# A wider second channel layer, computed in two parts, and a new order for stores and VectorE's work

## The chip, the cores and the metric

The kernel runs on one core of a Trainium2 chip. The metric is the device time of one execution in microseconds (us); lower is better. A core has TensorE (matmuls, "PE" in the profile), VectorE ("DVE"), ScalarE ("ACT"), GpSimd ("POOL") and SyncE ("SP", which here only issues DMA transfers).

## What is computed

Attention with a threshold for 8 batches and 8 heads, and behind it an MLP mixer. Everything is float32.

```python
# q, k, v: (8, 8, 576, 64); per batch and head
scores = (q @ k.T) / 8
thresh = scores.max(-1) - tau
scores = where(scores >= thresh, scores, -1e9)
attn = softmax(scores)
x = concat over heads of (attn @ v)          # (8, 576, 512), rows are tokens
# mixer: w_tok1 (576, 256), w_tok2 (256, 576), w_ch1 (512, 1536), w_ch2 (1536, 512)
h = relu(x.T @ w_tok1) @ w_tok2              # over tokens, per batch
u = x + h.T
out = u + relu(u @ w_ch1) @ w_ch2            # over channels, per token
```

The first channel layer is the product with w_ch1, the second channel layer the one with w_ch2. Adding u at the end is the residual.

## The kernel before

**Rows and rounds.** A batch is a row (b = 0 to 7). Attention is cut into units of 128 queries; two units make a round. A round is: scores on TensorE (L825, 24 passes of 64-row matmuls), row maxima on VectorE (L842, `mx`), the bias from them on GpSimd (L848), masks on ScalarE (L858), exponentials on ScalarE (L868), sums and reciprocals on VectorE (L276, L277), scaling on GpSimd (L285), a 32x32 block transpose of e on VectorE (L315, `T`), and four transfers on SP that bring the blocks to their places (L327, the "moves of e"). For three units the values (L365, L370) multiply with v.

**The mixer of the row before lies between.** While the attention of row b+1 runs, TensorE fills the time with the mixer of row b: transposes of x (L435), token layers (L454 and L472), then for one group of 256 tokens (two in row 0, none in row 7) the first channel layer (L948, 12 visits of 8 passes) and the second (L964, 2 x 4 visits of 24 passes). A float32 matmul shows as two passes. What is left of each row goes to DRAM (L531, "spill") and is computed in delayed groups at the end (L1309), where attention is over.

**Banks.** Token and channel visits, values and transposes share two PSUM banks (`m0`, `m1`). A visit takes a free bank, and an engine copies, clips or adds the result out of it; then the bank is free again. For the first channel layer this is a relu on ScalarE (L953) or VectorE (L956). For the second channel layer of rows 1 to 7 it is an add of the residual on VectorE (L978), for row 0 a copy on ScalarE (L984).

**The residual.** In rows above 0 the tokens of a group lie permuted and transposed. `turn_u` (L933, two transposes on VectorE) writes u into the tile `us`, eight transfers (`move_u`, L940) bring it to the tile `ut`. Then `us` is written a second time, by the adds `us = bank + ut`, and stored (L988), one transfer for each 128 tokens. `us` has one buffer: the next group's `turn_u` waits until both stores of the group before have landed.

**The order** is made when the program is built. A small planner (`Scheduler`) holds one clock for each engine and takes at each step the operation that can start earliest; among those that can start now, the one with the lower `rank`, then the older one. Each operation has a fixed cost; a transfer's landing is reckoned from the bytes at 214 KB per us and 1.5 us. Scores of later rounds are held back until as much mixer work is done as is due (`plan`, `done`). The planner only writes each engine's instruction list; on the chip each engine works strictly through its list and waits for semaphores.

Of the kernel before, what the change touches and what calls it, by code (L numbers as in the profile page):

```python
# [21 lines left out]
def kernel(  # L22
# [523 lines left out]

    TOKEN_RANK, TOKEN_AFTER_TOKEN = 1.5, 2.5
    SLACK, SPARE = 1.0, 4.0
    FLIGHT, RATE, LANDING = 8, 214.0, 1.5
    WARM_UNTIL, WARM_GAP, WARM_TURN = 110.0, 0.6, 0.11  # L550

    class Op:

        def __init__(self, eng, cost, fn, deps, after, rank, lag, row, index):
            self.eng, self.cost, self.fn, self.rank, self.lag, self.row, self.index = eng, cost, fn, rank, lag, row, index
            self.end, self.bank, self.frees, self.later, self.open, self.other = None, None, None, [], 0, None
            self.dmas, self.landed, self.shared = None, None, False
            self.deps = [d for d in deps if d is not None]
            for d in self.deps + [d for d in after if d is not None]:
                if d.end is None:  # L560
                    d.later.append(self)
                    self.open += 1
# [5 lines left out]
    class Scheduler:  # L568
# [22 lines left out]
        def banked(self, cost, work, on, cost_out, leave, deps=(), rank=5, row=None, rank_out=0, other=None):  # L591
# [3 lines left out]
            y.frees = x  # L595
            return x, y

        def sure(self, x):
            t = max([d.landed + SPARE if d.landed else d.end + d.lag + SLACK * (d.eng != x.eng) for d in x.deps] + [0.0])
            if x.bank:  # L600
                t = max(t, min(b.free for b in self.banks if b.free is not None) + SLACK)
            return t

        def start(self, x, eng):
            t = max([d.landed or d.end + (d.lag if d.eng != eng else 0.0) for d in x.deps] + [0.0])
            if x.dmas and len(self.in_flight) == FLIGHT:
                t = max(t, self.in_flight[0])
            if x.shared and eng == "dve":
                t = max(t, self.clock["pool"])
            if x.bank:  # L610
                frees = [b.free for b in self.banks if b.free is not None]
                if not frees:
                    return None
                t = max(t, min(frees))
            return max(t, self.clock[eng])
# [46 lines left out]
        def run(self, until):  # L662
            while not until():
                best = None
                for e in self.clock:
                    c = self.pick(e)
                    if c and (best is None or c[0][0] < best[0][0]):
                        best = c + (e,)
                if best is None:
                    assert all(x.end is not None for x in self.ops), [(x.eng, x.rank, x.index, x.open) for x in self.ops if x.end is None][:20]  # L670
                    return
                _, t, x, eng = best
                if eng == "pe" and t < WARM_UNTIL:
                    self.keep_warm(t)
                self.ready[x.eng].remove(x)
                if x.other:
                    self.ready[x.other[0]].remove(x)
                    if eng != x.eng:
                        x.eng, x.cost, x.fn = x.other
                if x.dmas:  # L680
                    x.end = self.transfer(t, *x.dmas)
                    x.landed = self.in_flight[-1]
                else:
                    x.end = t + x.cost
                self.clock[x.eng] = x.end
                if x.eng == "pe":
                    self.last_rank = x.rank
                if x.bank:
                    b = min((b for b in self.banks if b.free is not None), key=lambda b: b.free)
                    b.free = None  # L690
                    x.bank = b, b.pool.tile([P, MAIN], F32, tag=b.tag, name=f"bank_{x.index}")
                    x.fn(x.bank[1])
                    if x.row is not None:
                        self.done += x.cost
                elif x.frees:
                    b, tile_ = x.frees.bank
                    x.fn(tile_)
                    b.free = x.end + 0.15
                else:
                    x.fn()  # L700
                for y in x.later:
                    y.open -= 1
                    if not y.open:
                        self.enter(y)
# [214 lines left out]
    def make_groups(b, halves):  # L919
        uT = xTs[b]  # L920
        reads = []
        for i in range(NOW[b]):
# [32 lines left out]
            def relu_v(bank, j, s=s):  # L955
                nc.vector.tensor_scalar(out=s["g"][:, j, 0:n], in0=bank[:, 0:n], scalar1=0.0, scalar2=None, op0=ALU.max)  # L956

            def ch2(bank, t, c, s=s, i=i):
                to = bank[:, 0:P]
                t0 = GR * i + P * t  # L960
                if not b:
                    nc.tensor.matmul(to, lhsT=uT[:, c, t0 : t0 + P], rhs=ident, is_transpose=True, start=True, stop=False, skip_group_check=True)
                for j in range(NJ):
                    nc.tensor.matmul(  # L964
                        to,
                        lhsT=s["g"][:, j, P * t : P * t + P],
                        rhs=wc2[:, j, P * c : P * c + P],
                        start=(j == 0 and b > 0),
                        stop=(j == NJ - 1),
                        skip_group_check=True,  # L970
                    )

            def leave(bank, t, c, s=s):
                if not b and "us" not in s:
                    new_us(s)
                o = s["us"][:, t].rearrange("q a x -> q (a x)")[:, P * c : P * c + P]
                if b:
                    nc.vector.tensor_add(  # L978
                        out=o.rearrange("q (k d) -> q k d", k=4),
                        in0=bank[:, 0:P].rearrange("q (k d) -> q k d", k=4),  # L980
                        in1=s["ut"][:, t][:, :, 32 * c : 32 * c + 32],
                    )
                else:
                    nc.scalar.copy(out=o, in_=bank[:, 0:P])  # L984
# [5 lines left out]
            have = halves["20"] + (halves["21"] if i else [])  # L990
            moved = []
            if b:
                turn = sched.op("dve", 1.2, turn_u, have + state["stores"] + state["adds"] + (converted if b == 1 else []), 5)
                reads.append(turn)
                moved = [sched.op("sp", 1.2, lambda k=k, m=move_u: m(k), (turn,), 1, dmas=(nt, 53, 0.645)) for k in range(4)]
            relus = []
# [15 lines left out]
            seconds, stores, adds = [], [], []  # L1012
            for t in range(nt):
                outs = []
                for c in range(NCC):
                    x, y = sched.banked(
                        2.7 if b else 2.8,
                        lambda bank, t=t, c=c, f=ch2: f(bank, t, c),
                        "dve" if b else "act",
                        0.21,  # L1020
                        lambda bank, t=t, c=c, f=leave: f(bank, t, c),
                        relus + moved + (converted if not b else []) + (state["stores"] if not b else []),
                        2,
# [4 lines left out]
                    seconds.append(x)  # L1028
                    if not b:
                        reads.append(x)  # L1030
                    fills[b] = fills.get(b, 0.0) + x.cost
                adds += outs
                stores.append(sched.op("sp", 0.35, lambda t=t, f=store: f(t), outs, 2, dmas=(1, 150, 0.35)))
            state["ch2"], state["stores"], state["adds"] = seconds, stores, adds
        return reads

# [451 lines left out]
```

## Time and profile before

| | |
|---|---|
| median of 3 runs | 1270.09 us (1269.9 to 1276.9) |
| the profiled execution's own time | 1273.39 us |
| its span, first to last instruction | 1271.4 us |
| mean granted TensorE clock | 0.991 |
| TensorE busy / VectorE / ScalarE / GpSimd | 97% / 59% / 44% / 25% |
| second channel layer, matmuls (L964) | 1536 passes of 128 columns, 181.4 us busy |
| first channel layer, matmuls (L948) | 768 passes of 256 columns, 181.0 us busy |
| adds out of the bank (L978) | 48 of 128x128, 275 ns each |
| `turn_u` (L933) | 12 transposes, 1088 ns each |
| stores of groups and delayed groups (L988 and others), 256 KB | 32, 2.1 us from issue to landing in the median |

The profile is of one execution. Its page gives each engine's busy time, the groups of instructions by line of the kernel with count and mean duration, and who waited for whom. Busy time of TensorE is modelled at the ends of matmuls, so that the distance between two starts says more than the duration of one. The 16 stores at L988 are those of rows 0 to 6; the rest belong to the delayed groups. "SPq" is an issue of a transfer on SP.

### The profile page before, as it was taken

What the parts mean: (1) busy time and instruction counts of PE and PEld (TensorE: products, weight loads), DVE (VectorE), ACT (ScalarE), POOL (GpSimd) and SP (SyncE); (2) the same over time, 40 slices, a digit from 0 to 9 for tenths busy, and PEclk for the clock granted to TensorE, in tenths of its full rate; (3) what the DMA queues carried; (4) which work ended last, traced back from release to release, by engine and by line L of the source; (5) the groups of instructions that cost most, each with busy time, mean ns of one, the idle gap of its engine ahead of it and who ended that gap; (6) DMA issues with size and microseconds to landing.
All of it is one profiled execution on the core that took longest, in us unless ns stands there. A gap on an engine that the chain in (4) does not pass through costs nothing.

```text
span 1271.4 us, 21773 instructions
## 1 busy us (share of the span) xinstructions
PE 1237.8 (97%) x8150; PEld 1015.3 (80%) x8150; DVE 755.0 (59%) x1163; ACT 564.0 (44%) x1233; POOL 315.4 (25%) x518
## 2 busy tenths in 40 slices
PE   8888999999999999999989999999999999999998
PEld 7656778797678778878867777888988888888887
DVE  6699982656666667756666756761443534444443
ACT  6998862554645545556465455531110202011120
POOL 4565641232223333323323322410001010000100
PEclk9899999999999999999999999999999999999999
DMA  9546985366777786786776875750212101021011
GB/s 167 139 124 166 214 212 131 87 128 160 168 164 175 160 169 150 165 178 137 179 148 135 187 159 111 179 150 1 60 23 67 34 25 42 18 67 25 26 34 33
DMA packets 324216, 149.23 MB, mean 117 GB/s; under 512 B 223696, under 2 KB 316880, under 8 KB 324112
## 3 DMA queue, kind: packets, MB, share of 16 engines
q1 hardware_dynamic: 322240, 147.64, 50.5%
q8 instruction: 64, 1.05, 0.4%
q10 hardware_dynamic: 1872, 0.21, 0.1%
q14 instruction: 40, 0.33, 0.1%
HBM read 47.32 MB, written 13.50 MB: 48 GB/s over the span
## 4 chain that ended last, share of the span: by engine, by line
PE 78%; SPq 6%; DVE 5%; DMA 5%; ACT 4%; issue 2%; POOL 0%; DVEq 0%; ACTq 0%; POOLq 0%
PE bank L964 11%; PE bank L948 10%; PE o L1309 10%; PE sc L825 9%; PE bank L370 7%; PE hx L1309 6%; PE bank L454 5%; PE hmm L1309 4%; PE oz L1309 4%; PE hz L1309 4%; PE bank L472 4%; SPq L327 3%; PE bank L365 2%; DVE mx L842 2%; ACT e L858 2%
## 5 line engine op out<-in xcount | busy, mean ns | idle before, releaser
L285 POOL TENSOR_SCALAR e<-e,rr 128x576 f32<-128x576 f32 x288 | 213.2, 758 | 299.1 <-DVE rr L277 286.6
L858 ACT ACTIVATE e<-sc,bias 128x576 f32<-128x576 f32 x288 | 194.1, 740 | 156.8 <-POOL bias L848 155.1
L842 DVE TENSOR_REDUCE mx<-sc 128x2 f32<-128x1152 f32 x144 | 188.1, 1347 | 58.9 <-PE sc L825 58.4
L868 ACT ACTIVATE e<-e,ntau 128x576 f32<-128x576 f32 x288 | 220.4, 778 | 0.3
L315 DVE STREAM_TRANSPOSE T<-e 128x1152 f32<-128x1152 f32 x126 | 170.0, 1362 | 36.1 <-POOL e L285 22.2
L948 PE MATMUL bank<-xT,wc 128*128 128x256 f32 x768 | 181.0, 389 | 6.1 <-ACT g L953 5.1
L964 PEld LDWEIGHTS bank<-wc,g 128*128 128x128 f32 x1536 | 178.0, 192 | 10.4 <-issue 2.4
L964 PE MATMUL bank<-wc,g 128*128 128x128 f32 x1536 | 181.4, 276 | 0.9 <-DVE xT L483 0.4
L948 PEld LDWEIGHTS bank<-xT,wc 128*128 128x128 f32 x768 | 144.2, 192 | 36.6 <-ACT g L953 6.5
L825 PE MATMUL sc<-kT,qT 64*128 64x192 f32 (+1 forms) x1920 | 168.8, 337 | 2.7 <-ACT e L858 2.7
L825 PEld LDWEIGHTS sc<-kT,qT 64*128 64x128 f32 (+1 forms) x1920 | 140.8, 179 | 32.1 <-issue 16.3
L370 PE MATMUL bank<-eT,lv 128*64 128x384 f32 (+1 forms) x1024 | 135.2, 406 | 0.0
L1392 POOL TENSOR_TENSOR us<-us,ut 128x256 f32<-128x256 f32 x27 | 22.4, 843 | 391.8 <-DVE us L1230 391.8
L370 PEld LDWEIGHTS bank<-eT,lv 128*64 128x64 f32 x1024 | 74.4, 137 | 49.7 <-issue 41.3
L848 POOL TENSOR_SCALAR bias<-mx,toff 128x2 f32<-128x2 f32 x144 | 38.8, 270 | 197.9 <-DVE mx L842 193.3
L454 PE MATMUL bank<-x_sb,w 128*128 128x256 f32 x320 | 72.8, 383 | 0.3 <-DVE eT L305 0.2
L472 PE MATMUL bank<-w,a 128*128 128x192 f32 (+1 forms) x256 | 72.8, 418 | 0.2 <-DVE xT L483 0.2
L454 PEld LDWEIGHTS bank<-x_sb,w 128*128 128x128 f32 x320 | 59.8, 190 | 11.3 <-issue 1.3
L953 ACT ACTIVATE g<-bank 128x256 f32<-128x256 f32 x66 | 25.3, 383 | 92.9 <-PE bank L948 92.7
L1357 ACT ACTIVATE ga<-hmm 128x256 f32<-128x256 f32 x30 | 11.5, 384 | 116.8 <-PE hmm L1309 116.8
L1230 DVE TENSOR_TENSOR temps<-hx,temps 128x256 f32<-128x256 f32 x60 | 25.1, 418 | 56.7 <-PE hx L1309 56.6
L868 ACT ACTIVATION_READ_ACCUMULATOR e<-e,ntau 128x1 f32 x288 | 58.4, 203 | 0.0
(133 smaller groups left out, 1519.6 us busy)
## 6 DMA issues: line engine op xcount, KB each, us to landing
eT<-T SPq DMA_DIRECT2D x504, 144.0 KB, 3.0
lk<-in_k_dram SPq DMA_DIRECT2D x126, 72.0 KB, 2.9
lq<-in_q_dram SPq DMA_DIRECT2D x124, 72.0 KB, 3.1
out_dram<-us SPq DMA_DIRECT2D x32, 256.0 KB, 2.1
ut<-us SPq DMA_DIRECT2D x128, 64.0 KB, 2.1
lv<-in_v_dram SPq DMA_DIRECT2D x112, 72.0 KB, 2.6
spare<-in_moe_w_ch_dram SPq DMA_DIRECT2D x8, 512.0 KB, 3.9
extra<-in_moe_w_ch_dram SPq DMA_DIRECT2D x8, 512.0 KB, 3.8
```

What stands on the lines that cost most here:

```text
L285: nc.gpsimd.tensor_scalar(out=eh, in0=eh, scalar1=rr[:, h : h + 1], scalar2=1.0, op0=ALU.mult, op1=ALU.mult)
L315: nc.vector.transpose(out=T.rearrange("p a (c x) -> p c a x", c=NK), in_=e.rearrange("p (c a x) -> p c a x", c=NK, a=4))
L370: nc.tensor.matmul(to[r], lhsT=lv[:, j, :], rhs=e[j], start=False, stop=(c == NI - 1), skip_group_check=True)
L454: nc.tensor.matmul(to, lhsT=w1[:, t, P * m : P * m + P], rhs=x(t), start=(t == 0), stop=(t == NT - 1), skip_group_check=len(products) > 1,)
L472: nc.tensor.matmul(bank[:, n * i : n * i + n], lhsT=hidden[b][:, m, P * c : P * c + P], rhs=w2[:, m, lo : lo + n], start=(m == 0), stop=(m ...
L825: nc.tensor.matmul(sc[h][rows, f, HT * k : HT * k + HT], lhsT=qT[r, cols], rhs=kT[r, HT * f : HT * f + HT], start=True, stop=True, skip_gr ...
L842: nc.vector.tensor_reduce(out=mx[:, h], in_=sc[h][:, :, 0 : 2 * HT].rearrange("p f (k x) -> p k f x", k=2), axis=AX.XY, op=ALU.max)
L858: nc.scalar.activation(out=eh, in_=part[h], func=AF.Prelu, bias=bias[:, h], scale=SCALE, alpha=STEEP)
L868: nc.scalar.activation(out=eh, in_=eh, func=AF.Exp, bias=ntau, accum_out=rs[:, h, 0:1])
L948: nc.tensor.matmul(bank[:, 0:n], lhsT=wc1[:, j, c, :], rhs=uT[:, c, GR * i : GR * i + n], start=(c == 0), stop=(c == NCC - 1))
L964: nc.tensor.matmul(to, lhsT=s["g"][:, j, P * t : P * t + P], rhs=wc2[:, j, P * c : P * c + P], start=(j == 0 and b > 0), stop=(j == NJ - 1 ...
L1309: nc.tensor.matmul(ps, lhsT=l, rhs=r, start=start and x == 0, stop=x == len(pairs) - 1, skip_group_check=not start)
```

## The change

For rows above 0, a visit to the second channel layer now makes 256 of the 512 features instead of 128 (`wide = 2`). A group has 2 x 2 visits instead of 2 x 4, each of 12 matmuls with 256 columns. Each visit is two operations of the planner (`banked_in_two`): the first takes the bank and makes 6 of the 12 products, the second, with a slightly lower rank than the first, the other 6 in the same bank; between them the planner may put other work. One add on VectorE then takes 256 features out of the bank. Row 0 stays as it was.

Four numbers of the planner change with it. The store of a group's rows gets rank -1 instead of 2 on SP and is reckoned with 256 KB instead of 150. `turn_u` is reckoned with 2.05 us instead of 1.2. An operation of VectorE that needs a transfer is planned 2.0 us (`LATE`) after the reckoned landing, once TensorE's planned clock is over 200 us (`CALM`). The second part's cost is added to `done` by hand (`counts`).

```diff
--- before.py
+++ after.py
@@ -546,7 +546,7 @@
 
     TOKEN_RANK, TOKEN_AFTER_TOKEN = 1.5, 2.5
     SLACK, SPARE = 1.0, 4.0
-    FLIGHT, RATE, LANDING = 8, 214.0, 1.5
+    FLIGHT, RATE, LANDING, LATE, CALM = 8, 214.0, 1.5, 2.0, 200.0
     WARM_UNTIL, WARM_GAP, WARM_TURN = 110.0, 0.6, 0.11
 
     class Op:
@@ -554,7 +554,7 @@
         def __init__(self, eng, cost, fn, deps, after, rank, lag, row, index):
             self.eng, self.cost, self.fn, self.rank, self.lag, self.row, self.index = eng, cost, fn, rank, lag, row, index
             self.end, self.bank, self.frees, self.later, self.open, self.other = None, None, None, [], 0, None
-            self.dmas, self.landed, self.shared = None, None, False
+            self.dmas, self.landed, self.shared, self.counts = None, None, False, False
             self.deps = [d for d in deps if d is not None]
             for d in self.deps + [d for d in after if d is not None]:
                 if d.end is None:
@@ -595,6 +595,15 @@
             y.frees = x
             return x, y
 
+        def banked_in_two(self, cost, work, on, cost_out, leave, deps, rank, row, rank_out):
+            x = self.op("pe", cost, lambda bank: work(bank, 0), deps, rank, row=row)
+            z = self.op("pe", cost, lambda: work(x.bank[1], 1), (x,), rank - 0.1)
+            z.counts = True
+            y = self.op(on, cost_out, leave, (z,), rank_out, row=row)
+            x.bank = True
+            y.frees = x
+            return z, y
+
         def sure(self, x):
             t = max([d.landed + SPARE if d.landed else d.end + d.lag + SLACK * (d.eng != x.eng) for d in x.deps] + [0.0])
             if x.bank:
@@ -602,7 +611,8 @@
             return t
 
         def start(self, x, eng):
-            t = max([d.landed or d.end + (d.lag if d.eng != eng else 0.0) for d in x.deps] + [0.0])
+            late = LATE if eng == "dve" and self.clock["pe"] > CALM else 0.0
+            t = max([d.landed + late if d.landed else d.end + (d.lag if d.eng != eng else 0.0) for d in x.deps] + [0.0])
             if x.dmas and len(self.in_flight) == FLIGHT:
                 t = max(t, self.in_flight[0])
             if x.shared and eng == "dve":
@@ -698,6 +708,8 @@
                     b.free = x.end + 0.15
                 else:
                     x.fn()
+                    if x.counts:
+                        self.done += x.cost
                 for y in x.later:
                     y.open -= 1
                     if not y.open:
@@ -955,30 +967,32 @@
             def relu_v(bank, j, s=s):
                 nc.vector.tensor_scalar(out=s["g"][:, j, 0:n], in0=bank[:, 0:n], scalar1=0.0, scalar2=None, op0=ALU.max)
 
-            def ch2(bank, t, c, s=s, i=i):
-                to = bank[:, 0:P]
+            wide = 2 if b else 1
+
+            def ch2(bank, t, c, half=None, s=s, i=i, wide=wide):
+                to = bank[:, 0 : wide * P]
                 t0 = GR * i + P * t
                 if not b:
                     nc.tensor.matmul(to, lhsT=uT[:, c, t0 : t0 + P], rhs=ident, is_transpose=True, start=True, stop=False, skip_group_check=True)
-                for j in range(NJ):
+                for j in range(NJ) if half is None else range(NJ // 2 * half, NJ // 2 * half + NJ // 2):
                     nc.tensor.matmul(
                         to,
                         lhsT=s["g"][:, j, P * t : P * t + P],
-                        rhs=wc2[:, j, P * c : P * c + P],
+                        rhs=wc2[:, j, P * c : P * c + wide * P],
                         start=(j == 0 and b > 0),
                         stop=(j == NJ - 1),
                         skip_group_check=True,
                     )
 
-            def leave(bank, t, c, s=s):
+            def leave(bank, t, c, s=s, wide=wide):
                 if not b and "us" not in s:
                     new_us(s)
-                o = s["us"][:, t].rearrange("q a x -> q (a x)")[:, P * c : P * c + P]
+                o = s["us"][:, t].rearrange("q a x -> q (a x)")[:, P * c : P * c + wide * P]
                 if b:
                     nc.vector.tensor_add(
-                        out=o.rearrange("q (k d) -> q k d", k=4),
-                        in0=bank[:, 0:P].rearrange("q (k d) -> q k d", k=4),
-                        in1=s["ut"][:, t][:, :, 32 * c : 32 * c + 32],
+                        out=o.rearrange("q (w k d) -> q w k d", w=wide, k=4),
+                        in0=bank[:, 0 : wide * P].rearrange("q (w k d) -> q w k d", w=wide, k=4),
+                        in1=s["ut"][:, t].rearrange("q k (c d) -> q c k d", c=NCC)[:, c : c + wide],
                     )
                 else:
                     nc.scalar.copy(out=o, in_=bank[:, 0:P])
@@ -990,7 +1004,7 @@
             have = halves["20"] + (halves["21"] if i else [])
             moved = []
             if b:
-                turn = sched.op("dve", 1.2, turn_u, have + state["stores"] + state["adds"] + (converted if b == 1 else []), 5)
+                turn = sched.op("dve", 2.05, turn_u, have + state["stores"] + state["adds"] + (converted if b == 1 else []), 5)
                 reads.append(turn)
                 moved = [sched.op("sp", 1.2, lambda k=k, m=move_u: m(k), (turn,), 1, dmas=(nt, 53, 0.645)) for k in range(4)]
             relus = []
@@ -1012,12 +1026,13 @@
             seconds, stores, adds = [], [], []
             for t in range(nt):
                 outs = []
-                for c in range(NCC):
-                    x, y = sched.banked(
-                        2.7 if b else 2.8,
-                        lambda bank, t=t, c=c, f=ch2: f(bank, t, c),
+                for c in range(0, NCC, wide):
+                    make = sched.banked_in_two if b else sched.banked
+                    x, y = make(
+                        2.6 if b else 2.8,
+                        lambda bank, *half, t=t, c=c, f=ch2: f(bank, t, c, *half),
                         "dve" if b else "act",
-                        0.21,
+                        0.35 if b else 0.21,
                         lambda bank, t=t, c=c, f=leave: f(bank, t, c),
                         relus + moved + (converted if not b else []) + (state["stores"] if not b else []),
                         2,
@@ -1028,9 +1043,9 @@
                     seconds.append(x)
                     if not b:
                         reads.append(x)
-                    fills[b] = fills.get(b, 0.0) + x.cost
+                    fills[b] = fills.get(b, 0.0) + x.cost * wide
                 adds += outs
-                stores.append(sched.op("sp", 0.35, lambda t=t, f=store: f(t), outs, 2, dmas=(1, 150, 0.35)))
+                stores.append(sched.op("sp", 0.35, lambda t=t, f=store: f(t), outs, -1 if b else 2, dmas=(1, 256, 0.6)))
             state["ch2"], state["stores"], state["adds"] = seconds, stores, adds
         return reads
 
```

## The prediction, made before the changed kernel ran

> **What bounds the kernel now.** I read the page's busy shares first, then the stretches, then what TensorE waited for, and last the timeline around its longest waits.
>
> ```profile
> span 1271.4 us, 21773 instructions
> ...
> PE 1237.8 (97%) x8150; PEld 1015.3 (80%) x8150; DVE 755.0 (59%) x1163; ACT 564.0 (44%) x1233; POOL 315.4 (25%) x518
> ```
>
> TensorE (PE) is busy 97% of the span, and no other engine is above 59%. The view of stretches shows where the missing 3% lie (first number the stretch's length, then PE's busy time):
>
> ```profile
> 0.00:200.00 200.00, 184.65 (x1390) 141.52 (x1392) 162.80 (x264) 155.27 (x327) 105.23 (x163) 0.97 0.73 170
> ...
> 622.00:728.00 106.00, 102.75 (x759) 81.19 (x756) 70.24 (x102) 55.59 (x120) 30.82 (x54) 0.98 0.71 158
> 728.00:835.00 107.00, 104.44 (x777) 82.56 (x776) 70.46 (x98) 62.16 (x136) 33.15 (x59) 0.98 0.67 155
> ...
> 904.00:1271.00 367.00, 362.54 (x1680) 318.81 (x1678) 158.30 (x291) 54.40 (x130) 22.40 (x27) 1.00 0.15 39
> ```
>
> The first 200 us lose about 15 us, but the change has not begun there: in the built order the engines' first differences come after the first row, at some 290 to 300 us. The last 367 us (the delayed groups, 1680 passes at L1309) have no wait in them, and their code is untouched. What can move lies between 290 and 904 us. There TensorE is the bound, so a microsecond comes only from shorter matmuls or from fewer waits of TensorE. All that TensorE waited for between 200 and 904 us sums to 13.2 us in the view of waits (us in total, times, longest):
>
> ```profile
> PE bank L948 <- ACT g L953: 5.1, 3, 2.6
> PE bank L365 <- DMA x_sb<-extra: 1.9, 1, 1.9
> PE bank L962 <- DVE rr L276: 1.2, 1, 1.2
> PE bank L365 <- DVE xT L483: 1.0, 1, 1.0
> PE bank L365 <- DMA lv<-in_v_dram: 1.0, 2, 0.6
> ```
>
> The 1.2 us at L962 are in the first row and 0.4 us are at 903 us, which leaves 11.6 us within reach. The largest is a chain that begins in VectorE's queue:
>
> ```profile
> 631.60 0.59 SPq L988 DMA_DIRECT2D out_dram<-us  x1
> ...
> 634.41 2.08 DVE L933 STREAM_TRANSPOSE us<-xT 128x512 f32<-128x512 f32 x2 [3.95 <-DMA out_dram<-us]
> ...
> 636.42 1.33 DVE L315 STREAM_TRANSPOSE T<-e 128x1152 f32<-128x1152 f32 x1
> 637.68 2.58 DVE L842 TENSOR_REDUCE mx<-sc 128x2 f32<-128x1152 f32 x2
> ...
> 639.39 1.37 ACT L858 ACTIVATE e<-sc,bias 128x576 f32<-128x576 f32 x2 [3.94 <-POOL bias L848]
> ...
> 640.65 0.39 ACT L953 ACTIVATE g<-bank 128x256 f32<-128x256 f32 x1
> ...
> 641.09 3.55 PE L948 MATMUL bank<-xT,wc 128*128 128x256 f32 x8 [2.60 <-ACT g L953]
> ```
>
> Read it downwards. The store of a group (L988) went out at 631.60, though its last add had ended at 613.45: it stood in SP's queue behind other transfers. VectorE's next turn of u (L933) reuses the stored tile and stood 3.95 us waiting. Behind it on VectorE were a transpose of e and the row maxima (L842), which came late; ScalarE's masks (L858) wait for those, and the relu (L953) stands behind two masks. No bank was free until it, so TensorE stood 2.60 us. The same chain costs 2.08 us at 746 us.
>
> **The change, part by part.** *Wider matmuls.* For rows 1 to 6 (six groups) the second channel layer has 6 x 96 matmuls of 128 columns; each shows as two passes, 1152 in all. They become 288 matmuls of 256 columns, 576 passes (the built program has 288 matmuls fewer). The price of a pass is the distance between starts in stretches without waits:
>
> ```profile
> 866.16 1.89 PE L948 MATMUL bank<-xT,wc 128*128 128x256 f32 x8
> ...
> 867.88 4.48 PE L454 MATMUL bank<-x_sb,w 128*128 128x256 f32 x20
> ...
> 872.20 1.89 PE L948 MATMUL bank<-xT,wc 128*128 128x256 f32 x8
> ...
> 876.51 2.84 PE L964 MATMUL bank<-wc,g 128*128 128x128 f32 x24
> ...
> 879.19 1.46 PE L472 MATMUL bank<-w,a 128*128 128x384 f32 x4
> ```
>
> (879.19 - 876.51) / 24 = 111.7 ns for 128 columns, (872.20 - 866.16) / 28 = 215.7 ns for 256. So 1152 x 0.1117 = 128.7 becomes 576 x 0.2157 = 124.2: **-4.5 us**, all on the path. The Trainium skill, "TensorE: Matmul & The Clock Gate", section "Back-to-back issue gap", makes the warm gap columns/2.4 plus 2.5 ns, so merging two matmuls saves one fixed 2.5 ns. By that rule, even with two such gaps in each pass, 576 x 5 ns = 2.9 us would be an estimate of the gain, and the sum would be 1.6 us less favourable. The trace has 223.4 - 215.7 = 7.7 ns per merged pair of passes, and the measurement decides.
>
> *Two parts.* Each visit of 5.2 us is cut into two of 12 passes, 2.6 us, so the number of fillers between attention work stays 48. A filler next to attention's 64-row matmuls pays for the switch:
>
> ```profile
> 305.86 1.99 PE L948 MATMUL bank<-xT,wc 128*128 128x256 f32 x8
> 307.78 0.87 PE L365 MATMUL bank<-eT,vl 128*64 128x384 f32 x4
> ```
>
> 1.92 us from start to start, where the same eight passes took 1.72 above: 0.1 us a switch. The built order has 202 such switches in place of 196: **+0.6 us**. The planner counts a group as 12 x 1.79 + 8 x 2.6 = 42.3 us of work (before 43.1), so the due times of the scores hardly move.
>
> *The adds.* 48 adds of 128 columns become 24 of 256. The second form is in the trace:
>
> ```profile
> L978 DVE TENSOR_TENSOR us<-bank,ut 128x128 f32<-128x128 f32 x48 | 13.2, 275 | 34.6 <-PE bank L964 34.5
> L1230 DVE TENSOR_TENSOR us<-o,ut 128x256 f32<-128x256 f32 x10 | 4.2, 425 | 12.9 <-PE o L1309 12.9
> ```
>
> Two cost 0.55 us, one wide one 0.425, 3 us less on VectorE in all. I count 0: TensorE works in the other bank meanwhile (at least 1.3 us of it). Without that cover it would be 24 x 0.425 = 10.2 us.
>
> *The store first on SP, and later places for VectorE's work behind transfers.* In the built order the second store of a group moves, in the steady rows, from behind the spill, eight moves of e and four of x to ahead of them: 0.59 + 8 x 0.63 + 4 x 0.62 = 8.1 us earlier. Two transposes of e, two maxima, the turn of x, a relu and two transposes of q and k, more than 7 us, now stand between the group's last add and the turn of u; before there were some 3. A landing takes 2 to 4.6 us, so the turn should find its tile free, and the two waits go: 2.60 + 2.08 = **-4.7 us**. Should only half of the lateness go, it is -2.3. The price: spill, moves and loads are issued 0.59 us later once per store, twelve times. Values (L365) now wait for transfers 2.9 us in all; a delay of 0.59 that reached them in each of six groups would be +3.5. I take 0: TensorE waited for transfers at three of its 48 visits of values, so at the others there is slack.
>
> *The remaining waits.* After these two, 11.6 - 4.7 = 6.9 us of short waits remain, at places that the new plan reorders. Bounds: -6.9 (all go) to +6.9 (as many again). With two banks, the work that TensorE has between two uses of one bank says which way: reuses with under 1 us between them, past the first row's first layer, are 10 in the old order and 3 in the new, by such row prices. I take **-1.0**, near nothing, since most of these waits are of V for transfers and adds rather than for banks.
>
> The sum: -4.5 + 0.6 - 4.7 - 1.0 = -9.6 us. On the profiled execution (span 1271.4, its own time 1273.39, so 2.0 around it) that is a span of 1261.8. The median of the runs, 1270.1, is 3.3 below that execution's time; the same difference from it gives **1260.5 us**, 0.8% faster. A measurement of this kernel can tell about 1% from no change, here 12.7 us.
>
> **The rivals.** *One wait for another.* The stall moves instead of going: the turn of u, placed later, delays what is next on VectorE (maxima or transposes of e), and the 4.7 + 1.0 us are given back elsewhere. For it: the planner places by fixed costs, and VectorE waits 28.9 us for v's loads as well. Against: in the trace the turn ends at 636 us and the first add of its group comes some 30 us later. Time: 1270.1 - 4.5 + 0.6 = 1266.2.
>
> *All waits go.* The plan, now closer to real store and turn times, leaves TensorE no wait after 290 us: 1270.1 - 3.9 - 11.6 = 1254.6. For it: rows 3 and 4 have nearly the same order, with wider bank distances. Against: rows 1 and 2 are irregular, and V waits for transfers there.
>
> *The held bank.* Of two banks one is now held through both parts and what stands between. If each of the 24 holds makes TensorE wait for one copy of values out of the other bank (0.48 us), it is +11.5: 1260.5 + 11.5 = 1272.0. The bank distances speak against it. The Trainium skill, "PSUM — Partial Sum Buffer", section "Summary: rules for kernel authors", says to evacuate promptly, which speaks for it; no run here shows a held bank yet.
>
> *SP's head is blocked: slower.* SP works strictly down its list. A store planned right after its add stands at the head when the add is late, and the moves of e behind it, which the values need, wait too. Today the stores are issued 6 to 20 us after their groups' adds, so they never block. If the add comes one pair of maxima late (2.6 us) at both stores of all six groups and TensorE waits for it each time, that is 12 x 2.6 = 31.2: 1260.5 + 31.2 = 1291.7. The kernel is slower than before from 0.8 us a store, and by over 1% from 1.9 us. Against: values are reached late, and TensorE waits for them only 3.9 us in all today.
>
> **How the numbers follow.** My forecast, with its own range 1257.5 to 1264, has 0.42; one wait for another 0.23; the held bank 0.07; these three lie within 1%, 0.72. All waits gone, with what lies near it, 0.20: faster by over 1% (below 1257.4). SP's blocked head 0.08: slower by over 1%. The range 1254 to 1275 reaches from all waits gone to the held bank with the 3.5 us of late transfers on top (1275.5), and leaves out the blocked head and the edge of the second case.
>
> **What would show each step.** Right: the second layer's passes start 216 ns apart and number 576 for rows 1 to 6; stores leave within a few us of the last add; VectorE's wait for the store (17.4 us now) is nearly gone; no wait above 2 us of L948 for the relu; the last 367 us unchanged. Wrong: a wait of SP for the adds with moves of e behind it, values waiting longer for transfers, or waits of TensorE after 290 us that sum to more than 11.6 us again.

## The result: 0.7% faster, within what was forecast

| | before | changed |
|---|---|---|
| median of 6 runs each | 1271.89 us | 1263.73 us (1261.59 to 1264.47) |
| ratio of runs, 95% interval | | 0.993 (0.991 to 0.995) |
| profiled execution: span | 1271.4 us | 1262.4 us |

The forecast was 1260.5 us, its own range 1257.5 to 1264, and "within 1%" had the chance 0.72. It started from a median of 1270.1 us for the kernel before; over the six runs here that median is 1271.89, so the gain is 8.2 us where 9.6 were forecast. The page of the changed kernel:

```profile
span 1262.4 us, 20603 instructions
...
PE 1229.3 (97%) x7574; PEld 990.0 (78%) x7574; DVE 754.5 (60%) x1140; ACT 563.6 (45%) x1232; POOL 315.8 (25%) x518
```

TensorE is as busy as before, with 576 passes fewer. Line numbers have moved: the first channel layer is now L960, the second L978, its add L992, the turn of u L945, the store L1002.

**A cleaner measure than the span.** The first 230 us, which the change does not touch, take between 229 and 236 us in the profiles of this study. I therefore also use the stretch from the first token layer of row 0's second half to the first delayed group. In the timelines of TensorE, before and changed, it begins and ends here:

```profile
233.31 2.86 PE L454 MATMUL bank<-x_sb,w 128*128 128x256 f32 x12
...
903.67 1.13 PE L1309 MATMUL hmm<-u,wc 128*128 128x256 f32 x4 [0.38 <-DVE us L978]
```

```profile
232.34 3.94 PE L454 MATMUL bank<-x_sb,w 128*128 128x256 f32 x17
...
894.72 1.03 PE L1324 MATMUL hmm<-u,wc 128*128 128x256 f32 x4
```

670.4 us before, 662.4 us changed: 8.0 us less, nearly all of the 8.2 us between the medians. (The two spans differ by 9.0 us; the other 1.0 lies ahead of the stretch.) The delayed groups behind it take the same time to their last pass: 362.5 and 362.4 us. A stretch is still the figure of one execution, and executions differ: on one chip those of the kernel before lay between 1263.6 and 1277.6 us.

**What went as planned.** Wide passes and the wide add, by form and shape, and two visits in the timeline:

```profile
L978 PE MATMUL bank<-wc,g 128*128 128x256 f32 x576 | 132.8, 380 | 0.0
...
L992 DVE TENSOR_TENSOR us<-bank,ut 128x256 f32<-128x256 f32 x24 | 9.8, 410 | 26.4 <-PE bank L978 26.4
```

```profile
864.52 2.75 PE L978 MATMUL bank<-wc,g 128*128 128x256 f32 x12
867.11 4.48 PE L454 MATMUL bank<-x_sb,w 128*128 128x256 f32 x20
```

(867.11 - 864.52) / 12 = 215.8 ns for a pass, 410 ns for the add. The chain behind the turn of u is gone. Timeline of the place that held the 2.60 us wait before:

```profile
621.01 0.42 DVE L992 TENSOR_TENSOR us<-bank,ut 128x256 f32<-128x256 f32 x1 [1.94 <-PE bank L978]
...
621.90 0.61 SPq L1002 DMA_DIRECT2D out_dram<-us  x1
622.61 1.29 SPq L531 DMA_DIRECT2D spill<-xT  x1
624.00 6.65 SPq L327 DMA_DIRECT2D eT<-T  x8
628.70 2.08 DVE L945 STREAM_TRANSPOSE us<-xT 128x512 f32<-128x512 f32 x2
```

The store leaves 0.5 us after its add, ahead of the spill and the moves of e, and the turn 7 us later finds its tile free. The view of VectorE's waits has 17.4 us for landed stores before, and now:

```profile
DVE us L945 <- DMA out_dram<-us: 1.8, 1, 1.8
```

**What did not.** What TensorE waited for from 200 us to the delayed groups:

```profile
PE bank L365 <- DMA eT<-T: 10.8, 3, 7.0
PE bank L976 <- DVE rr L276: 1.1, 1, 1.1
PE bank L960 <- DVE g L968: 0.3, 1, 0.3
```

The 5.1 us of waits for the relu and nearly all short ones are gone, but values (L365) now wait 10.8 us for moves of e, 7.0 us of it in one place in row 1. The timeline there:

```profile
329.04 2.48 SPq L412 DMA_DIRECT2D x_sb<-extra  x4
329.82 2.82 DVE L315 STREAM_TRANSPOSE T<-e 128x1152 f32<-128x1152 f32 x2 [0.51 <-POOL e L285]
...
331.56 3.58 SPq L952 DMA_DIRECT2D ut<-us  x4
...
333.90 2.22 PE L837 MATMUL sc<-kT,qT 64*128 64x192 f32 x24
...
335.24 7.76 SPq L327 DMA_DIRECT2D eT<-T  x12
...
343.15 1.55 PE L365 MATMUL bank<-eT,vl 128*64 128x384 f32 x4 [7.02 <-DMA eT<-T]
...
344.45 4.61 PE L370 MATMUL bank<-eT,lv 128*64 128x384 f32 x16
```

Two blocks of e are turned by 332.64, but SP is then issuing four of the transfers that bring u to `ut`, to 335.14. Only then do the moves of e go out, eight of them in 5.1 us, and land near 343. TensorE has nothing else: the scores end at 336, and no visit of the first channel layer is left to stand between them and the values. In the kernel before one stood there, and the values waited 1.88 us:

```profile
335.54 1.99 PE L948 MATMUL bank<-xT,wc 128*128 128x256 f32 x8
339.41 0.87 PE L365 MATMUL bank<-eT,vl 128*64 128x384 f32 x4 [1.88 <-DMA x_sb<-extra]
```

The wait in the changed kernel costs more than its length. The view of stretches (length, PE busy, then at the end granted clock, share of the DMA engines and GB/s):

```profile
336.00:343.00 7.00, 0.13 (x2) 0.00 (x0) 4.71 (x4) 4.54 (x9) 1.39 (x4) 0.88 0.85 203
343.00:348.30 5.30, 5.15 (x18) 2.22 (x20) 0.00 (x0) 1.12 (x4) 0.00 (x0) 0.51 0.73 167
```

At a clock of 0.51 the values take 4.61 us instead of 2.78; 5.1 us at half speed lose about 2.5 us. The kernel before paid in the same coin, which I had overlooked: behind its two waits for the relu the clock was halved too.

```profile
641.09:644.20 3.11, 3.11 (x7) 2.52 (x8) 1.20 (x2) 3.11 (x7) 0.00 (x0) 0.50 0.69 177
...
746.38:750.10 3.72, 3.72 (x10) 2.58 (x12) 1.50 (x3) 3.72 (x9) 0.00 (x0) 0.54 0.81 182
```

That is 1.6 and 1.7 us lost. In the trace's clock record half speed lasts 3.41 us each time before, and 6.83 us in the changed kernel. The Trainium skill, "TensorE: Matmul & The Clock Gate", section "What's actually happening", gives a free-running window of 3413 ns. The trace agrees: 3.41 and 6.83 us are one and two such windows.

### The profile page after: what moved, and what is told of

Same layout as the page of the kernel before. It is cut to its first block, busy times and chain, and to the rows that moved or that the text cites. A ratio compares the mean times of both kernels' runs of the same rounds, so it can differ in the third digit from the quotient of the medians.

```text
span 1262.4 us, 20603 instructions
## 1 busy us (share of the span) xinstructions
PE 1229.3 (97%) x7574; PEld 990.0 (78%) x7574; DVE 754.5 (60%) x1140; ACT 563.6 (45%) x1232; POOL 315.8 (25%) x518
## 4 chain that ended last, share of the span: by engine, by line
PE 81%; SPq 4%; DVE 4%; ACT 3%; DMA 2%; issue 1%; POOL 0%; DVEq 0%; POOLq 0%; ACTq 0%
PE bank L978 11%; PE bank L960 11%; PE o L1324 10%; PE sc L837 10%; PE bank L370 7%; PE hx L1324 6%; PE bank L454 6%; PE bank L472 5%; PE oz L1324 4%; PE hz L1324 4%; PE hmm L1324 4%; SPq L327 3%; PE bank L365 2%; DVE mx L854 1%; ACT e L870 1%
## 5 line engine op out<-in xcount | busy, mean ns | idle before, releaser
L978 PE MATMUL bank<-wc,g 128*128 128x256 f32 (+1 forms) x960 | 178.1, 338 | 0.0
L960 PE MATMUL bank<-xT,wc 128*128 128x256 f32 x768 | 175.8, 383 | 0.3 <-DVE g L968 0.3
L978 PEld LDWEIGHTS bank<-wc,g 128*128 128x128 f32 x960 | 152.3, 191 | 21.5 <-issue 3.8
L837 PEld LDWEIGHTS sc<-kT,qT 64*128 64x128 f32 (+1 forms) x1920 | 140.2, 179 | 32.7 <-issue 17.4
L960 PEld LDWEIGHTS bank<-xT,wc 128*128 128x128 f32 x768 | 143.0, 190 | 28.8 <-issue 6.1
L1372 ACT ACTIVATE ga<-hmm 128x256 f32<-128x256 f32 x30 | 11.5, 383 | 117.1 <-PE hmm L1324 117.1
L472 PEld LDWEIGHTS bank<-w,a 128*128 128x128 f32 x256 | 43.1, 189 | 20.1 <-issue 4.8
```

The source lines that it names most:

```text
L472: nc.tensor.matmul(bank[:, n * i : n * i + n], lhsT=hidden[b][:, m, P * c : P * c + P], rhs=w2[:, m, lo : lo + n], start=(m == 0), stop=(m ...
L837: nc.tensor.matmul(sc[h][rows, f, HT * k : HT * k + HT], lhsT=qT[r, cols], rhs=kT[r, HT * f : HT * f + HT], start=True, stop=True, skip_gr ...
L960: nc.tensor.matmul(bank[:, 0:n], lhsT=wc1[:, j, c, :], rhs=uT[:, c, GR * i : GR * i + n], start=(c == 0), stop=(c == NCC - 1))
L978: nc.tensor.matmul(to, lhsT=s["g"][:, j, P * t : P * t + P], rhs=wc2[:, j, P * c : P * c + wide * P], start=(j == 0 and b > 0), stop=(j == ...
```

## The experiments

My theory after the result: the narrow passes are worth about 4.5 us; the early store and the later turn remove the waits for the relu together with their low clock; against this stands a new wait for moves of e with its own low clock. The rivals: that the wide visits alone, or the planner's numbers alone, make the gain, and that the moves of e are late for another reason. "Stretch" is the measure above (before 670.4, changed 662.4 us), from one profile each; the time is a median, and the ratio, with its 95% interval, is against the kernel before on the same chip. Its medians there lay between 1268.6 and 1271.2 us, so ratios, not times, are to be compared between experiments (the changed kernel: 0.993, 0.991 to 0.995).

**1. Narrow passes in the changed order.**

```diff
-    nc.tensor.matmul(to, ..., rhs=wc2[:, j, P * c : P * c + wide * P], start=(j == 0 and b > 0), ...)
+    for w in range(wide):
+        nc.tensor.matmul(to[:, P * w : P * w + P], ..., rhs=wc2[:, j, P * c + P * w : P * c + P * w + P],
+                         start=(j == 0 and b > 0 and w == 0), ...)
```

> The changed kernel with its order untouched, but each matmul of 256 columns in the second channel layer of rows above 0 issued as two of 128 columns (1152 passes again in place of 576). My theory: the wide pass saves 7.7 ns per merged pair of passes, 576 x 7.7 ns = 4.5 us on the path, so this runs at 1263.7 + 4.5 = 1268.2 us, a ratio of about 0.997 to the kernel before, and the passes start 112 ns apart. Rival (the Trainium skill, TensorE: Matmul & The Clock Gate, Back-to-back issue gap, a fixed gap of 2.5 ns per matmul): 1.4 to 2.9 us, that is 1265.1 to 1266.6 us. A third possibility is that TensorE waits elsewhere for longer visits, above 1269 us.

Measured: 1269.4 us, ratio 0.9993 (0.9976 to 1.0011), stretch 668.1. The passes, from its timeline:

```profile
872.70 2.84 PE L979 MATMUL bank<-wc,g 128*128 128x128 f32 x24
875.38 4.48 PE L454 MATMUL bank<-x_sb,w 128*128 128x256 f32 x20
```

(875.38 - 872.70) / 24 = 111.7 ns. From start to next start, all passes of the second channel layer in the stretch take 154.3 us here and 149.4 in the changed kernel: the width is worth **4.9 us** in this pair of profiles (4.4 us by the price of a pass). The 1.4 to 2.9 us that the expectation worked out from the Trainium skill, "TensorE: Matmul & The Clock Gate", section "Back-to-back issue gap", which gives its formula for the isolated gap of one matmul, are too little for these float32 passes. The stretch is 5.7 us longer, since TensorE also waits 0.9 us more in it, so the third possibility has a small part in the result. The expected ratio of 0.997 lies just outside the interval: without the width the rest of the change gains little, and the interval holds 1.

**2. TensorE kept busy through the 7.0 us wait.**

```diff
+        if (b, p0, g) == (2, 2, 2):
+            for _ in range(60):
+                nc.tensor.transpose(out=bank[:, 0:P], in_=ident, identity=ident)
```

> The changed kernel with 60 transposes of the identity (0.11 us each, 6.6 us) put on TensorE ahead of the one visit of values that waited 7.0 us at 336 us; nothing else is changed. My theory: that wait costs 7.0 us and then 2.6 us more, because the granted clock is 0.51 for the 5.3 us behind it. With TensorE kept busy the clock stays at 1.0 and only the wait is left: 2.6 us less, 1261.1 us. Rival: the low clock does not come from the idle time, and the kernel stays at 1263.7 us or gets slower by what the transposes overrun the wait (up to 1 us).

Measured: 1264.4 us, 0.9952 (0.9933 to 0.9971), stretch 663.5. Its timeline:

```profile
336.80 6.77 PE L357 MATMUL bank<-ident 128*128 128x128 f32 x60
344.30 0.87 PE L368 MATMUL bank<-eT,vl 128*64 128x384 f32 x4 [0.73 <-issue]
344.97 2.78 PE L373 MATMUL bank<-eT,lv 128*64 128x384 f32 x16
```

The mechanism is as expected: kept busy, TensorE does the values in 2.78 us, not 4.61. The gain did not show. In this execution a wait of 2.2 us at 650 us was followed by 3.41 us at half speed; the changed kernel had a like wait there (2.3 us) without it. So the low clock is shown to come from the idle time, but a saving of 2.6 us in the whole is not.

**3. The later places from 400 us on.**

```diff
-    FLIGHT, RATE, LANDING, LATE, CALM = 8, 214.0, 1.5, 2.0, 200.0
+    FLIGHT, RATE, LANDING, LATE, CALM = 8, 214.0, 1.5, 2.0, 400.0
```

> The changed kernel with CALM 400 in place of 200, so that VectorE's work behind transfers gets its later places only from 400 us on. Row 1 then keeps a filler visit between the scores and the values at 336 us, as in the kernel before. My theory: the 7.0 us wait and the 2.6 us of low clock shrink to the 2 us that the kernel before has there, about 7.5 us less: 1256 us, a ratio of 0.988. Rival: the wait only moves to another visit of values (the transfers are late whatever stands before them), 1262 to 1266 us.

Measured: 1260.7 us, 0.9927 (0.9899 to 0.9955), stretch 662.1. The wait in row 1 fell to 3.5 us with no low clock behind it, but values in the next row waited 2.8 us at 447 us, with 3.41 us at half speed. The time is that of the changed kernel within the intervals; the 7.5 us that were expected did not come. The rival described it better: the wait partly moved.

**4. The widening alone.** LATE 0, and the old numbers for the turn of u and the store:

```diff
-stores.append(sched.op("sp", 0.35, ..., outs, -1 if b else 2, dmas=(1, 256, 0.6)))
+stores.append(sched.op("sp", 0.35, ..., outs, 2, dmas=(1, 150, 0.35)))
```

> Only the widening in two parts: the store's rank and size, the cost of turn_u and LATE are as before the change. My theory: the narrower passes go (-4.5 us, +0.6 for switches) and the waits behind the turn of u stay, so 1271.9 - 3.9 = 1268 us, a ratio of 0.997, and VectorE waits over 10 us in all for landed stores. Rival: the coarser visits alone remove the waits, 1259 to 1263 us, and VectorE's wait for stores is gone too.

Measured: 1265.4 us, 0.996 (0.9939 to 0.998), stretch 662.7. VectorE's waits for stores, and two of TensorE's waits:

```profile
DVE us L945 <- DMA out_dram<-us: 7.1, 3, 4.6
```

```profile
PE bank L365 <- DMA x_sb<-extra: 3.3, 1, 3.3
...
PE bank L978 <- ACT g L965: 0.9, 2, 0.6
```

The median lies between the two theories, and the interval holds the first one's 0.997. Coarser visits alone cut VectorE's wait for stores from 17.4 to 7.1 us, but did not remove it. TensorE's waits for ScalarE's relus fell all the same, from 5.1 us to the 0.9 shown. Values in row 1 wait 3.3 us, against 1.9 before, with LATE at 0: some of that wait is not LATE's. As this interval overlaps that of the changed kernel, it is not shown that the planner's numbers add anything to the widening.

**5. The early store alone,** in the kernel before:

```diff
-outs, 2, dmas=(1, 150, 0.35)
+outs, -1 if b else 2, dmas=(1, 256, 0.6)
```

> The kernel before with one edit: the store of a group gets rank -1 on SP and is reckoned with 256 KB. No widening, no LATE, old cost of turn_u. My theory: the store leaves within a few us of its last add, VectorE's 17.4 us of waiting for landed stores falls under 4 us, TensorE's two waits behind the relu (2.6 and 2.1 us) go, and the time falls by about 4.7 us: 1266.5 us, ratio 0.996. Rival: the store takes the place of moves of e, values wait instead, and the time stays at 1271 us.

Measured: 1267.4 us, 0.9991 (0.9974 to 1.0008), stretch 664.9. What TensorE waited for behind 200 us, and VectorE's wait for stores:

```profile
PE bank L365 <- DMA x_sb<-extra: 3.2, 1, 3.2
PE bank L365 <- DVE g L956: 1.7, 1, 1.7
...
PE bank L948 <- ACT g L953: 0.4, 1, 0.4
```

```profile
DVE us L933 <- DMA out_dram<-us: 10.1, 5, 3.8
```

The waits for the relu fall from 5.1 to 0.4 us with the store alone. In place of the expected "under 4 us", VectorE waits 10.1 us for stores: the turn still stands early in its list, but TensorE no longer waits long for a relu. Values wait 4.9 us in the lines shown, where they waited 3.9 us in all before, and behind the 3.2 us the clock was at half speed for 3.41 us. The early store is therefore enough to end the waits for the relu in this trace, and part of that is given back. The two measures part here: 5.5 us less in the stretch, but 1.1 us by the ratio, whose interval holds 1. The profiled execution of this run lay 1.9 us below its median, and that of the kernel before 1.5 us above its own, so the stretch probably makes the gain too large.

**6. The transfers to `ut` of row 1 from ScalarE's queue.**

```diff
-nc.sync.dma_start(out=s["ut"][:, m, k, :], ...)
+(nc.scalar if b == 1 else nc.sync).dma_start(out=s["ut"][:, m, k, :], ...)
```

> The changed kernel, every list as it is, but the eight transfers that bring u to ut in row 1 are issued from ScalarE in place of SP. My theory: the 7.0 us wait of values at 336 us comes from SP: four of these transfers (3.6 us of issue) stand ahead of the moves of e that the values need, because the turn of u has a later place. Without them on SP the moves start 2.5 to 3.6 us earlier, the wait falls to about 3.4 to 4.5 us and the low clock behind it may go: 3 to 6 us less than the changed kernel, 1258 to 1261 us. Rival: the moves are late because the transposes of e are (ScalarE and GpSimd ahead of them), so the wait stays at 7 us and the time at 1263.7.

Measured: 1261.0 us, 0.9938 (0.9915 to 0.996), stretch 660.1. Timeline:

```profile
330.70 2.82 DVE L315 STREAM_TRANSPOSE T<-e 128x1152 f32<-128x1152 f32 x2 [1.39 <-POOL e L285]
...
332.11 9.42 SPq L327 DMA_DIRECT2D eT<-T  x12
...
333.77 2.22 PE L837 MATMUL sc<-kT,qT 64*128 64x192 f32 x24
...
340.54 1.55 PE L365 MATMUL bank<-eT,vl 128*64 128x384 f32 x4 [4.55 <-DMA eT<-T]
```

The moves begin at 332.11 instead of 335.24, although the blocks of e are turned 0.9 us later, and the wait falls from 7.02 to 4.55 us: SP's queue was the cause of that part. What is left begins with the turned block: SP now issues its moves as soon as it is there. The low clock stayed, 6.83 us long, where the expectation had hoped that it would go. The twelve moves take 9.42 us here instead of 7.76, but 1.1 us of it is SP waiting for the third block; the eight that the values wait for take 5.8 us instead of 5.1. The ratio cannot be told from the changed kernel's.

**7 and 8. LATE 1.0 and LATE 0,** the rest of the change as it is (in the line of experiment 3, `2.0` becomes `1.0` or `0.0`).

> The changed kernel with LATE 1.0 in place of 2.0. Row 1 keeps a filler visit between scores and values. My theory: the 7.0 us wait falls to 2 to 4 us, the turn of u still finds its tile free, and the time is 1256 to 1260 us. Rival: with less margin the turn of u waits for landed stores again (over 5 us of VectorE) and the time is 1263 to 1266 us.

> The changed kernel with LATE 0: widening, early stores and the larger cost of turn_u stay. My theory: early stores alone free the tile in time, so TensorE's waits behind the relu stay away and the 7.0 us wait does not appear: 1259 to 1262 us, no slower than the changed kernel. Rival: LATE is what removes the waits; without it the waits behind the relu return (2 to 5 us) and the time is 1266 us or more.

Measured: with 1.0, 1261.4 us, 0.9947 (0.993 to 0.9965), stretch 661.5; with 0, 1264.8 us, 0.9963 (0.9943 to 0.9984), stretch 665.3. The wait in row 1 falls to 3.2 and 2.2 us in the two, with a visit of the first channel layer ahead of it again. With LATE 1.0 neither forecast time came. With LATE 0 the waits are many and short instead, the largest:

```profile
PE bank L454 <- DVE x_sb L439: 2.2, 2, 1.6
PE bank L978 <- DVE g L968: 2.2, 1, 2.2
PE bank L365 <- DMA x_sb<-extra: 2.2, 1, 2.2
PE bank L365 <- DVE g L968: 2.1, 2, 1.4
```

The full list sums to 15.8 us, against 12.6 in the changed kernel. No turn of u waits for long (3.2 us in all) and the 7.0 us wait does not appear, so my theory holds there, but its time of 1259 to 1262 us was missed. Waits behind relus did return, nearly all on VectorE (L968) and 5.9 us in all, as the rival has it, though its 1266 us was missed too. In these traces LATE removes short waits for VectorE and brings one long wait for moves; by the ratios the two cannot be told apart.

**9. Half of the last moves of a row from ScalarE's queue.**

```diff
-nc.sync.dma_start(out=turned_e[key][:, place, i, :], ...)
+on = nc.scalar if p0 and t >= 2 * GU and i % 2 else nc.sync
+on.dma_start(out=turned_e[key][:, place, i, :], ...)
```

> The changed kernel, but of the moves of e for the last three units of a row (the ones that the last values of the row need) every second one is issued from ScalarE's queue in place of SP's. Nothing else changes. My theory: values wait for SP's issue time (eight moves in 5.1 us), so half of them on another queue shortens the 7.0 us wait by about 2.5 us and the shorter ones at 512 and 650 us to under 1 us each: 4 us less than the changed kernel, 1260 us, ratio 0.990. Rival: ScalarE stands behind these moves' own waits, masks and relus get late, and TensorE waits there instead: 1264 us or more.

Measured: 1265.5 us, 0.9962 (0.9944 to 0.9979), stretch 660.7. The long wait is 5.5 us, 1.5 less and not 2.5, and from 200 us on TensorE waits 3.2 us more for relus and copies of ScalarE (0.9 and 0.2 us of it inside the stretch). So the theory came true in part, and the time is the rival's.

**10. One part instead of two.**

```diff
-make = sched.banked_in_two if b else sched.banked
+make = sched.banked
-    2.6 if b else 2.8,
+    5.2 if b else 2.8,
```

(and the sum `fills` takes this cost once instead of twice).

> The changed kernel with each visit of 256 columns as one operation of 24 passes (planned with 5.2 us) instead of two parts. My theory: the passes cost the same, there are half as many fillers, so that attention's visits find nothing to stand between them: TensorE waits 4 to 10 us more for values and scores than in the changed kernel, 1266 to 1272 us. Rival: the number of fillers does not matter, and with fewer switches (0.1 us each) the time is 1261 to 1264 us.

Measured: 1264.2 us, 0.9946 (0.9929 to 0.9964), stretch 665.1. Its trace has 4.7 us of values waiting for v, which the changed kernel has not, and a second low clock at 451 us. By the stretch it is 2.7 us slower than the changed kernel; the ratios' intervals overlap, and the median of 1264.2 us lies just above the rival's range. The worth of the two parts is open.

**11. Everything but the widening.**

```diff
-wide = 2 if b else 1
+wide = 1
```

(with the single visits and their old costs).

> The changed kernel without the widening: visits of 128 columns as before, with the early stores, the larger cost of turn_u and LATE 2.0. My theory: the waits behind the relu are gone (-4.7 us), but the 7.0 us wait of row 1 and its 2.6 us of low clock stay, as they come from LATE: about the time before, 1270 us, ratio 0.998 to 1.002. Rival: the planner's numbers are what makes the kernel faster, 1263 to 1265 us.

Measured: 1267.9 us, 0.9982 (0.9965 to 0.9999), stretch 666.3. From its view of TensorE's waits:

```profile
PE bank L365 <- DMA eT<-T: 6.7, 1, 6.7
PE bank L960 <- DVE g L968: 1.6, 3, 1.0
```

As expected: without the widening little is left, and the long wait is there without it, with 6.83 us of low clock. With experiments 7 and 8 this shows that LATE, not the wide visits, makes the wait so long.

**12. Both reliefs of SP together** (the edits of 6, for all rows, and of 9).

> The changed kernel with both relieved queues: the transfers to ut of all rows and every second move of e of a row's last three units are issued from ScalarE. My theory: each alone shortened the 7.0 us wait (to 4.5 and 5.5 us); together it falls to about 3 us, the waits at 512 and 650 us under 1 us, and from the first token layer behind 230 us to the delayed groups it takes 657 to 659 us (changed kernel 662.4): ratio about 0.989 to the kernel before. Rival: the low clock stays and ScalarE's masks get later by the issues, so that the stretch takes 660 to 663 us and the ratio is 0.992 to 0.995.

Measured: 1265.0 us, 0.9962 (0.9943 to 0.9982), stretch 661.7. The long wait is 3.7 us, but 6.83 us at half speed come with it as before, and from 200 us on TensorE waits 2.6 us for ScalarE's relus and copies elsewhere (1.4 us of it inside the stretch). The rival's stretch was right, and its ratio nearly. No version here is clearly faster than the changed kernel.

## Why the prediction was right, and where it was not

The width did what was forecast. The rest came near its forecast by luck: two wrong steps, one too small and one that took a cost as nothing, nearly cancel.

- **Width, -4.5.** Right: 4.9 by experiment 1.
- **Switches, +0.6, and the add at no cost.** The add took 410 ns (425 forecast), and no wait of TensorE for a bank held through two parts is in the list, so the rival of the held bank did not come. The switches were not measured by themselves.
- **The turn of u, -4.7.** The waits went. Experiment 5 shows that the early store alone does it, and experiment 4 that the widening alone does it too, though VectorE then still waits 7.1 us for stores. The term was too small for this pair of profiles: each wait had a low clock behind it, together 3.3 us, which no step of the sum held. One figure in it was misread: the add that ended at 613.45 was the last but one; the last ended at 620.7, so that the store left 10.9 us after it. Over all twelve stores it was 0 to 11 us, not 6 to 20; the changed kernel has 0 to 3.3.
- **Later transfers at no cost, and the remaining waits, -1.0.** This is the step that failed. The prediction took 0 for moves of e that reach the values late, because most visits of values had slack. Values waited 3.9 us before; they wait 10.8 us for moves of e now, with 2.5 us of low clock behind the longest wait. I had priced "one wait for another" at 5.7 us, as the place of the turn on VectorE; it came as 13.3 us. Of the 7.0 us, 2.5 came through the transfers to `ut` that the later turn puts ahead of the moves on SP (experiment 6), where I had listed SP's delay by the store itself (0.59 us) and not that of these transfers (3.6 us). The lost visit between scores and values is another part: with LATE 1.0 or 0 it stands there again and the wait is 3.2 or 2.2 us. The split beyond that is open. The other short waits nearly went: without the values, 0.7 us are left. The passes of x's transposes take 8.8 instead of 11.6 us from start to next start, of which the view of waits lists only 0.5 us; what shortened them was not tested.
- **The sum, in this pair of profiles.** Listed waits 11.6 to 11.5 (-0.1), low clock 3.3 to 2.5 (-0.8), x's transposes -2.3 beyond the listed waits, width -4.9, switches +0.6 (as forecast, not measured): -7.5 of the measured -8.0. My -9.6 came from other parts: too little taken away, and too little added.
- **By the ratios,** which rest on more runs: the change gains 0.7%, the widening alone 0.4%, the changed order with narrow passes 0.07%, everything but the widening 0.2%, the early store alone 0.1%. So no part of the reordering is worth much by itself, and the 4.7 us that the prediction gave to the early store and the later turn did not show without the width.
- **Rivals and signs.** SP's head was not blocked: SP stood 39.9 us at stores that waited for their adds, but all except 0.7 us of it in row 6's last two stores, behind attention's last moves. "All waits go" failed at row 1, as its own objection said. Of the signs of being wrong that the prediction named, one came, values waiting longer for transfers, and the sum of TensorE's waits, 11.5 us, missed its limit of 11.6 only just.

## What to carry to other kernels

When one engine is busy nearly all the time, list its waits one by one and follow each to the queue in which it begins; the cure of one is often a change of order in a queue, and everything that the moved step issues moves with it. Look at the granted clock behind each wait as well: here a wait of 2 us could cost 3.7. And a pass that is twice as wide cost 1.93 times a narrow one, a small gain, but one that every trace shows, while the gains from reordering mostly cancelled. One profile is one execution: before a gain is counted from it, compare its time with the median of the runs.

## What the runs showed beside it

- The clock fell to half after waits of TensorE as short as 2.1 to 2.9 us in some executions and not after 3.5 us in another (experiment 3). In the seven profiles in which the values of row 1 waited 3.7 us or more, half speed lasted 6.83 us there each time. Length alone does not decide for the short ones.
- A second queue shortened waits by less than the issue time that it took over. In the 7 us before the late values the DMA engines were 0.85 busy at 203 GB/s, and the eight moves took 5.8 us to issue in experiment 6 against 5.1. That the engines' load is the reason was not tested by itself.
